# Later block transposes of e, and x turned on VectorE: two changes to attention followed by an MLP mixer on one core

## The chip, the core and the metric

The kernel runs on one NeuronCore of a Trainium2 chip. Five engines work side by side, each through its own instructions in order: TensorE (PE: matrix products, and transposes against an identity), VectorE (DVE), ScalarE (ACT), GpSimd (POOL) and SyncE (SP), which here only issues DMAs. Semaphores order them. SBUF is the working memory of 128 partitions, PSUM holds the results of PE. The metric is the time of one execution on the device, in microseconds. Before the change its median over eight runs is 1392.33 us (1391.53 to 1393.89).

## The reference

Threshold attention over 8 batch rows, 8 heads, 576 tokens and 64 columns a head; then the heads are laid side by side to 512 columns, and an MLP mixer follows, first over tokens and then over channels.

```python
def _attn_ref(q, k, v, tau):
    scale = 1.0 / np.sqrt(q.shape[-1])
    scores = scale * np.matmul(q, k.transpose(0, 1, 3, 2))
    thresh = np.max(scores, axis=-1, keepdims=True) - tau
    scores = np.where(scores >= thresh, scores, -1000000000.0)
    scores = scores - np.max(scores, axis=-1, keepdims=True)
    attn = np.exp(scores)
    attn = attn / (np.sum(attn, axis=-1, keepdims=True) + 1e-09)
    return np.matmul(attn, v)

def _moe_ref(x, w_tok1, w_tok2, w_ch1, w_ch2):
    xt = x.transpose(0, 2, 1)                      # x: (8, 576, 512)
    h = np.maximum(xt @ w_tok1, 0.0) @ w_tok2      # 576 -> 256 -> 576
    u = x + h.transpose(0, 2, 1)
    h2 = np.maximum(u @ w_ch1, 0.0) @ w_ch2        # 512 -> 1536 -> 512
    return u + h2
```

## The kernel before

**Units.** Attention is cut into 144 units: a batch row b has two halves w of two head pairs, and a half has nine units t. Eight units take 128 queries of one head pair (two heads); unit t = 4 takes the last 64 queries of both pairs of the half. A loop (L534) runs over the units and some rounds more, and its source order is the order in which each engine gets its instructions (`manual_schedule`, L81). Round u does, in this order:

- `scores(u)` (L287): 8 or 16 products into two PSUM tiles sc, the maxima mx on DVE (L306), a bias on POOL.
- `norm(u-1)` (L327): reciprocals rr on DVE, e scaled by rr on POOL.
- for unit w = u-2 the turn of e. In batch row 0, `turn` (L345): PE transposes with copies by DVE or ACT. From batch row 1 on, `turn_blocks` (L361): one DVE transpose in 32x32 blocks of 128x1152 into T (L368), and after the second unit of a group (a group is two units, or the unit t = 4 alone) 16 DMAs on SP (L378), which move the blocks across partitions into eT. The product with v follows two rounds later.
- `fill(0.4)` (L566): MLP steps, see below.
- `weigh(u)` (L310): threshold by a Prelu and exponential on ACT, with three times `fill(0.2)` between.
- issues of q and k loads for a pair two ahead (L576), two DMAs in each of the first eight units of a half, on SP in batch row 0 and on ACT later; lq and lk have two buffers (L70). `prep` at t = 2 and t = 7 turns a loaded pair on DVE into qT and kT (L283).
- `values` (L390), for what is due: products with v into pv (L408, L413), copied by ACT into xT (L418), which holds x with columns on partitions, two batch rows in one tile.

Between these stand calls of `weight(n)` (L223). It loads a weight piece in 64-bit form on SP (L176) into one of four raw buffers and decodes it on ACT, DVE and POOL; L191, L193, L201, L205, L209 and L215 are that decoding. It ends near 190 us.

**MLP steps.** When the last product of a batch row is emitted, `push(b)` (L515) queues its MLP as a list of steps with costs in us, mixed with what is left of the list before; `fill(share)` emits steps worth that share of a quota per round. The quota spreads the list over UB - 1 = 17 rounds and keeps 45 us for the time after the next push. The steps are: five `turn_x(t)` (four PE transposes of xT into PSUM, L430, and an ACT copy into x_sb, L431, which has tokens on partitions and one buffer); two `tok1(m)` (five products of w1 and x_sb, L439, Relu into a on ACT, L440); eight `tok2(c, f)` (two products, L446, and an add into xT on DVE, L450); then for groups of 256 tokens twelve `ch1` (L468, Relu into g on ACT, L469) and eight `ch2` (transposes of u, L480, products, L484; the last one of four copies to o on DVE, L489, and stores on SP, L490). The products of the MLP share two PSUM buffers, ps_mm; pv, x and the transposes share two, ps_tr.

```python
        for i, step in enumerate(steps):
            n = 2 if i in (NT, NT + NTK) else 1
            todo.extend(old[:n] + [step])
            del old[:n]
        todo.extend(old)
```

Of the kernel before, what the change touches and what calls it, by code (L numbers as in the profile page):

```python
# [9 lines left out]
F32 = mybir.dt.float32  # L10
# [11 lines left out]
def kernel(  # L22
# [71 lines left out]
    VL = 4  # L94
    vlast = [const.tile([P, P], F32, name=f"vl{i}") for i in range(VL)]

    def load_qk(n, eng, part=None):


        b, p = pairs[n]  # L100
        if n not in loaded:
            loaded[n] = [ld.tile([P, S // 32, 32], F32, tag=tag, name=f"{tag}_{n}") for tag in ("lq", "lk")]
        for i in range(4) if part is None else (part,):
            h, c = divmod(i, 2)
            for src, t, on in zip((q, k), loaded[n], eng):
                on.dma_start(
                    out=t[32 * i : 32 * i + 32], in_=src[b, 2 * p + h, :, 32 * c : 32 * c + 32].rearrange("(n t) d -> t n d", t=32)
                )

    def load_v(n):  # L110

# [127 lines left out]
        weight(3 * i + 4 - steps_done)  # L239

    load_piece(0)
    load_qk(1, (nc.sync, nc.sync))
    load_v(0)
    for i in range(1, NRAW):
        load_piece(i)
# [29 lines left out]
    def in_blocks(b):  # L275
        return b > 0
# [84 lines left out]
    def turn_blocks(u):  # L361

        key, place, n = group_of(u)
        e = st.pop(u)
        if place == 0:
            Ts[key] = work.tile([P, NK * 2 * P], F32, tag="T", name=f"T_{u}")
        T = Ts[key][:, 0 : NK * n * P]
        nc.vector.transpose(  # L368
            out=T.rearrange("p (a c n x) -> p c a n x", a=4, c=NK, n=n)[:, :, :, place, :],
            in_=e.rearrange("p (c a x) -> p c a x", c=NK, a=4),  # L370
        )
        if place == n - 1:
            del Ts[key]
            eTs[key] = work.tile([P, NK * 2 * P], F32, tag="eT", name=f"eT_{u}")
            w = NK * n * 32
            for a in range(4):
                for i in range(4):
                    nc.sync.dma_start(  # L378
                        out=eTs[key][32 * a : 32 * a + 32, w * i : w * i + w], in_=T[32 * i : 32 * i + 32, w * a : w * a + w]
                    )  # L380
# [37 lines left out]
        nc.scalar.copy(out=x, in_=ps)  # L418


    def token_mlp(b):
        xT = xTs.pop(b)
        o = S * (b % 2)
        s = {}

        def turn_x(t):
            M = MT[t]
            ps = ps_tr.tile([P, MAIN], F32, tag="tr", name=f"tx_{b}_{t}").rearrange("p (c x) -> p c x", c=NP)
            for p in range(NP):
                nc.tensor.transpose(out=ps[0:M, p, :], in_=xT[:, p, o + t * P : o + t * P + M], identity=ident)  # L430
            nc.scalar.copy(out=x_sb[0:M, t, :], in_=ps[0:M].rearrange("q p d -> q (p d)"))  # L431

        def tok1(m):
            need(2)
            if m == 0:
                s["a"] = work.tile([P, NTK, DM], F32, tag="a", bufs=1, name=f"a_{b}")
            ps = ps_mm.tile([P, DM], F32, tag="mm", name=f"t1_{b}_{m}")
            for t in range(NT):
                nc.tensor.matmul(ps, lhsT=w1[:, t, P * m : P * m + P], rhs=x_sb[:, t, :], start=(t == 0), stop=(t == NT - 1))  # L439
            nc.scalar.activation(out=s["a"][:, m, :], in_=ps, func=AF.Relu)  # L440

        def tok2(c, f):
            need(6)
            ps = ps_mm.tile([P, HS], F32, tag="mm", name=f"t2_{b}_{c}_{f}")
            for m in range(NTK):
                nc.tensor.matmul(  # L446
                    ps, lhsT=s["a"][:, m, P * c : P * c + P], rhs=w2[:, m, HS * f : HS * f + HS], start=(m == 0), stop=(m == NTK - 1)
                )
            u = xT[:, c, o + HS * f : o + HS * f + HS]
            nc.vector.tensor_add(out=u, in0=u, in1=ps)  # L450

        steps = [(0.44, lambda t=t: turn_x(t)) for t in range(NT)]
        steps += [(4.3, lambda m=m: tok1(m)) for m in range(NTK)]
        steps += [(0.97, lambda c=c, f=f: tok2(c, f)) for c in range(NCC) for f in range(2)]
        return steps
# [59 lines left out]
    def push(b):  # L515
        nonlocal quota
        uT = xTs[b]
        steps, old = token_mlp(b), list(todo)
        todo.clear()

        for i, step in enumerate(steps):
            n = 2 if i in (NT, NT + NTK) else 1
            todo.extend(old[:n] + [step])
            del old[:n]
        todo.extend(old)
        for i in range(2) if b % 2 == 0 else range(2, (2 * S + GR - 1) // GR):
            todo.extend(channel_mlp(b - b % 2, uT, i))
        quota = (sum(c for c, _ in todo) - (KEEP if b else KEEP_FIRST)) / (UB - 1)

    prep(0)  # L530
    due = deque()
    b_now = 0
# [86 lines left out]
```

## Time and profile before

| what | us |
|---|---|
| median of eight runs | 1392.33 |
| the profiled execution | 1391.53 |
| its span in the trace | 1389.70 |
| rounds without MLP (batch row 0): first matmul at | 8.89 |
| last product of scores at | 1185.4 |
| last matmul ends near | 1385.9 |

The span is that of the instructions in the trace; 1.8 us of the execution lie around it. Groups of instructions that matter here, as busy us and mean ns of one:

```profile
L368 DVE STREAM_TRANSPOSE T<-e 128x1152 f32<-128x1152 f32 x126 | 172.5, 1369 | 16.4 <-DMA eT<-T 9.7
L418 ACT COPY xT<-pv 128x256 f32<-128x256 f32 x64 | 23.8, 372 | 161.9 <-PE pv L413 155.9
...
L446 PE MATMUL t<-w,a 128*128 128x288 f32 x256 | 76.4, 426 | 14.9 <-DVE xT L450 11.7
L439 PE MATMUL t<-x_sb,w 128*128 128x512 f32 x160 | 72.9, 602 | 0.7 <-ACT g L469 0.7
```

A line gives the source line, the engine, the operation, its output and input tiles with shapes and the count; then the busy time in us and the mean of one in ns; then how long the engine had idled before these instructions in total, and who ended most of that. Two further groups, from the list of all groups: the x transposes (L430) are 160 with 26.5 us busy, and the x_sb copies (L431) are 40 with 23.1 us. An engine that idles costs time only if it is the one that the others wait for, so the stretches have to be told apart before these figures mean anything.

### The profile page before, as it was taken

To read this page: it belongs to the slowest core of one execution; us is meant where nothing else is said; L and a number is where in the kernel's file an instruction comes from. 1 tells how busy PE (TensorE), PEld (TensorE's weight loads), DVE (VectorE), ACT (ScalarE), POOL (GpSimd) and SP (SyncE) were. 2 spreads that over 40 slices of the span, in tenths; PEclk is the share of its full clock that TensorE was granted. 3 is DMA by queue.
4 is the path that set the end of the run, shared out by engine and by line. 5 is a ranking of instruction groups with operands and counts; after the bars stand their busy time and mean duration, and the time that the engine had idled before them with its cause. 6 is when DMAs were issued, how large, how long until landed. Compare 5 with 4: busy or idle time off the path is not lost.

```text
span 1389.7 us, 19515 instructions
## 1 busy us (share of the span) xinstructions
PE 1324.9 (95%) x6866; PEld 831.3 (60%) x6866; DVE 586.4 (42%) x1009; ACT 590.5 (42%) x1328; POOL 359.3 (26%) x683
## 2 busy tenths in 40 slices
PE   6776799999999999999999999999999999999998
PEld 3444465646565666665766567565657566575675
DVE  5789874444444444434244444433343453101000
ACT  5776564444454344443444435353434444120110
POOL 4566553232222122212122222221221222000000
PEclk9997999999999999999999999999999999999999
DMA  6444754444444433433433444443433433300000
GB/s 134 99 111 124 189 142 120 107 121 94 106 117 108 106 87 96 109 86 77 111 85 91 105 96 102 99 105 78 100 92 89 103 74 86 84 8 16 8 8 23
DMA packets 257376, 128.34 MB, mean 92 GB/s; under 512 B 208064, under 2 KB 221376, under 8 KB 257280
## 3 DMA queue, kind: packets, MB, share of 16 engines
q1 hardware_dynamic: 131632, 111.46, 30.6%
q10 hardware_dynamic: 125648, 15.64, 7.1%
q8 instruction: 55, 0.90, 0.3%
q14 instruction: 41, 0.34, 0.1%
HBM read 43.25 MB, written 9.44 MB: 38 GB/s over the span
## 4 chain that ended last, share of the span: by engine, by line
PE 85%; DVE 6%; SPq 2%; DMA 2%; POOL 2%; ACT 1%; issue 1%; ACTq 0%; DVEq 0%; POOLq 0%
PE c L484 27%; PE c L468 25%; PE sc L301 11%; PE pv L413 7%; PE t L439 5%; PE t L446 3%; DVE mx L306 3%; PE pv L408 2%; SPq L378 2%; PE tx L430 1%; PE c L480 1%; PE pv_s L413 1%; DVE T L368 1%; DMA scratch<-in_moe_w_ch_dram 1%; ACT e L316 1%
## 5 line engine op out<-in xcount | busy, mean ns | idle before, releaser
L306 DVE TENSOR_REDUCE mx<-sc 128x1 f32<-128x576 f32 x288 | 204.7, 751 | 522.5 <-PE sc L301 520.5
L468 PE MATMUL c<-xT,wc 128*128 128x256 f32 (+1 forms) x1920 | 399.0, 361 | 1.1 <-ACT g L469 0.9
L484 PE MATMUL c<-wc,g 128*128 128x512 f32 x864 | 389.1, 596 | 0.0
L468 PEld LDWEIGHTS c<-xT,wc 128*128 128x128 f32 x1920 | 334.2, 190 | 70.9 <-issue 28.4
L307 POOL TENSOR_SCALAR bias<-mx,toff 128x1 f32<-128x1 f32 x288 | 80.1, 278 | 812.4 <-DVE mx L306 757.9
L316 ACT ACTIVATE e<-sc,bias 128x576 f32<-128x576 f32 x288 | 199.3, 740 | 157.6 <-POOL bias L307 157.2
L484 PEld LDWEIGHTS c<-wc,g 128*128 128x128 f32 x864 | 157.9, 190 | 175.3 <-issue 173.2
L469 ACT ACTIVATE g<-c 128x256 f32<-128x256 f32 (+1 forms) x240 | 86.8, 362 | 334.3 <-PE c L468 329.6
L334 POOL TENSOR_SCALAR e<-e,rr 128x576 f32<-128x576 f32 x288 | 219.3, 774 | 15.8 <-DVE rr L331 3.8
L323 ACT ACTIVATE e<-e,ntau 128x576 f32<-128x576 f32 x288 | 220.6, 771 | 0.0
L301 PE MATMUL sc<-kT,qT 64*128 64x288 f32 (+1 forms) x1280 | 190.4, 436 | 15.5 <-DVE kT L283 8.9
L368 DVE STREAM_TRANSPOSE T<-e 128x1152 f32<-128x1152 f32 x126 | 172.5, 1369 | 16.4 <-DMA eT<-T 9.7
L301 PEld LDWEIGHTS sc<-kT,qT 64*128 64x128 f32 (+1 forms) x1280 | 104.3, 180 | 91.1 <-issue 47.7
L413 PE MATMUL pv<-eT,lv 128*64 128x256 f32 x1024 | 124.5, 386 | 0.0
L413 PEld LDWEIGHTS pv<-eT,lv 128*64 128x64 f32 x1024 | 75.5, 139 | 37.8 <-issue 1.1
L418 ACT COPY xT<-pv 128x256 f32<-128x256 f32 x64 | 23.8, 372 | 161.9 <-PE pv L413 155.9
L489 DVE COPY o<-c 128x512 f32<-128x512 f32 x36 | 24.5, 680 | 160.8 <-PE c L484 160.8
L446 PE MATMUL t<-w,a 128*128 128x288 f32 x256 | 76.4, 426 | 14.9 <-DVE xT L450 11.7
L439 PE MATMUL t<-x_sb,w 128*128 128x512 f32 x160 | 72.9, 602 | 0.7 <-ACT g L469 0.7
L446 PEld LDWEIGHTS t<-w,a 128*128 128x128 f32 x256 | 45.3, 191 | 41.7 <-DVE xT L450 19.5
L450 DVE TENSOR_TENSOR xT<-xT,t 128x288 f32<-128x288 f32 x64 | 28.0, 440 | 80.4 <-PE t L446 80.2
L323 ACT ACTIVATION_READ_ACCUMULATOR e<-e,ntau 128x1 f32 x288 | 56.4, 196 | 0.0
(48 smaller groups left out, 604.3 us busy)
## 6 DMA issues: line engine op xcount, KB each, us to landing
eT<-T SPq DMA_DIRECT2D x896, 72.0 KB, 2.0
scratch<-in_moe_w_ch_dram SPq DMA_DIRECT2D x24, 512.0 KB, 4.1
lv<-in_v_dram SPq DMA_DIRECT2D x32, 288.0 KB, 3.4
out_dram<-o SPq DMA_DIRECT2D x36, 256.0 KB, 2.2
eT<-T SPq DMA_DIRECT2D x224, 36.0 KB, 1.9
lk<-in_k_dram ACTq DMA_DIRECT2D x108, 72.0 KB, 2.7
lq<-in_q_dram ACTq DMA_DIRECT2D x104, 72.0 KB, 2.1
lq<-in_q_dram SPq DMA_DIRECT2D x24, 72.0 KB, 3.4
```

Source lines behind the costliest of these rows:

```text
L301: nc.tensor.matmul(sc[h][rows, f, 0:HS], lhsT=qT[r, cols], rhs=kT[r, HS * f : HS * f + HS], start=True, stop=True)
L306: nc.vector.tensor_reduce(out=mx[:, c], in_=sc[h][:, :, 0:HS], axis=AX.XY, op=ALU.max)
L316: nc.scalar.activation(out=eh, in_=sc[h][:, :, 0:HS], func=AF.Prelu, bias=bias[:, h : h + 1], scale=SCALE, alpha=STEEP)
L323: nc.scalar.activation(out=eh, in_=eh, func=AF.Exp, bias=ntau, accum_out=rs[:, h : h + 1])
L334: nc.gpsimd.tensor_scalar(out=eh, in0=eh, scalar1=rr[:, h : h + 1], scalar2=1.0, op0=ALU.mult, op1=ALU.mult)
L368: nc.vector.transpose(out=T.rearrange("p (a c n x) -> p c a n x", a=4, c=NK, n=n)[:, :, :, place, :], in_=e.rearrange("p (c a x) -> p c a ...
L413: nc.tensor.matmul(to[r], lhsT=lv[:, j, :], rhs=eT[:, j], start=False, stop=(c == NI - 1), skip_group_check=True)
L439: nc.tensor.matmul(ps, lhsT=w1[:, t, P * m : P * m + P], rhs=x_sb[:, t, :], start=(t == 0), stop=(t == NT - 1))
L446: nc.tensor.matmul(ps, lhsT=s["a"][:, m, P * c : P * c + P], rhs=w2[:, m, HS * f : HS * f + HS], start=(m == 0), stop=(m == NTK - 1))
L468: nc.tensor.matmul(ps, lhsT=wc1[:, j, c, :], rhs=uT[:, c, GR * i : GR * i + n], start=(c == 0), stop=(c == NCC - 1))
L469: nc.scalar.activation(out=s["g"][:, j, 0:n], in_=ps, func=AF.Relu)
L484: nc.tensor.matmul(flat, lhsT=s["g"][:, j, P * t : P * t + P], rhs=wc2[:, j, :], start=False, stop=(j == NJ - 1), skip_group_check=True)
```

## The change

It has two named parts and three that come with them.

1. `turn_blocks(w)` is called after `fill(0.4)` instead of ahead of it (batch row 0 keeps its `turn` where it was).
2. For b > 1, x is no longer turned by `turn_x`. After the last product of each half of a batch row (p odd, c = 1), an entry goes to `moves`. One round later `turn_x_blocks` turns the half's two pairs of xT in 32x32 blocks by one DVE instruction of 128x1152 into xt (one buffer). In each of the four rounds after it `move_x` issues four DMAs, two on SP and two on ACT, that put the blocks into x_sb. One round later still, after the second half, `push(b)` queues the MLP, now without `turn_x` steps. The columns of x_sb stand in another order, so the copies of batch rows 0 and 1 and the Relu of `tok1` permute them.
3. lq and lk have one buffer. The q and k loads are issued in other rounds: what a pair needs in the rounds between two `prep` calls. Pair 1 is loaded in rounds 0 and 1 rather than ahead of the loop.
4. The quota after `push(1)` spreads its list over UB + 4 = 22 rounds, since the next push comes later.
5. The loop has six rounds more at its end.

```diff
-            loaded[n] = [ld.tile([P, S // 32, 32], F32, tag=tag, name=f"{tag}_{n}") for tag in ("lq", "lk")]
+            loaded[n] = [ld.tile([P, S // 32, 32], F32, tag=tag, bufs=1, name=f"{tag}_{n}") for tag in ("lq", "lk")]
...
     load_piece(0)
-    load_qk(1, (nc.sync, nc.sync))
     load_v(0)
...
+    x_read = {}
+
+    def x_in_blocks(b):
+        return b > 1
+
+    def x_columns(t, M):
+        return x_sb[0:M, t, :].rearrange("q (i p d) -> q p i d", i=4, p=NP)
+
+    def turn_x_blocks(b, w):
+        xt = work.tile([P, S // 32 * 64], F32, tag="xt", bufs=1, name=f"xt_{b}_{w}")
+        o = S * (b % 2)
+        nc.vector.transpose(
+            out=xt.rearrange("q (c p d) -> q p c d", c=S // 32, p=2),
+            in_=xTs[b][:, 2 * w : 2 * w + 2, o : o + S].rearrange("q p (c r) -> q p c r", r=32),
+        )
+        return xt.rearrange("q (c x) -> q c x", x=64)
+
+    def move_x(b, w, xt, i):
+        if w == 0 and i == 0:
+            assert b < 1 or x_read[b - 1]
+        for a in range(4):
+            n = len(range(a, S // 32, 4))
+            eng = nc.scalar if a % 2 else nc.sync
+            eng.dma_start(
+                out=x_sb[32 * a : 32 * a + 32, 0:n, P * i + 64 * w : P * i + 64 * w + 64], in_=xt[32 * i : 32 * i + 32, a::4, :]
+            )
...
-            nc.scalar.copy(out=x_sb[0:M, t, :], in_=ps[0:M].rearrange("q p d -> q (p d)"))
+            nc.scalar.copy(out=x_columns(t, M), in_=ps[0:M].rearrange("q p (i d) -> q p i d", i=4))
...
-        steps = [(0.44, lambda t=t: turn_x(t)) for t in range(NT)]
+        steps = [] if x_in_blocks(b) else [(0.44, lambda t=t: turn_x(t)) for t in range(NT)]
...
-            n = 2 if i in (NT, NT + NTK) else 1
+            n = 2 if len(steps) - i in (8, 10) else 1
...
-        quota = (sum(c for c, _ in todo) - (KEEP if b else KEEP_FIRST)) / (UB - 1)
+        quota = (sum(c for c, _ in todo) - (KEEP if b else KEEP_FIRST)) / (UB + 4 if b == 1 else UB - 1)
...
-    for u in range(len(units) + LAG + 4):
+    for u in range(len(units) + LAG + 10):
...
-            if in_blocks(key[0]):
-                turn_blocks(w)
-            else:
+            if not in_blocks(key[0]):
                 for i in range(3):
                     turn(w, i)
...
         if b_now:
             fill(0.4)
+        if back and in_blocks(key[0]):
+            turn_blocks(w)
...
-            m = n + 2 + t // 4
-            if t < 8 and m < len(pairs):
-                load_qk(m, (nc.scalar if b_now else nc.sync,) * 2, t % 4)
-                if t % 4 == 3:
-                    load_v(m)
+            when = {3: (2, 0, 2), 4: (2, 2, 4), 5: (2, 4, 6), 6: (2, 6, 8), 8: (3, 0, 3), 0: (1, 3, 6), 1: (1, 6, 8)}
+            if u == 0:
+                load_qk(1, (nc.sync, nc.sync), range(0, 3))
+            if t in when:
+                m, lo, hi = when[t]
+                if n + m < len(pairs):
+                    load_qk(n + m, (nc.scalar if b_now else nc.sync,) * 2, range(lo, hi))
+            if t in (3, 7) and n + 2 + t // 4 < len(pairs):
+                load_v(n + 2 + t // 4)
...
+        for m in list(moves):
+            at, b, qd = m
+            if u == at:
+                xts = turn_x_blocks(b, qd)
+            elif u < at + 5:
+                move_x(b, qd, xts, u - at - 1)
+            else:
+                moves.remove(m)
+                if qd == 1:
+                    push(b)
         while due and due[0][0] <= u:
             _, b, p, c = due.popleft()
             values(b, p, c)
-            if p == NP - 1 and c == 1:
-                push(b)
+            if c == 1 and p % 2:
+                if x_in_blocks(b):
+                    moves.append((u + 1, b, p // 2))
+                elif p == NP - 1:
+                    push(b)
```

More of the change, by code (lines that the diff above doesn't have):

```diff
@@ L95, with load_qk @@
     vlast = [const.tile([P, P], F32, name=f"vl{i}") for i in range(VL)]
-    def load_qk(n, eng, part=None):
+    def load_qk(n, eng, parts=range(8)):
         b, p = pairs[n]
         if n not in loaded:
-            loaded[n] = [ld.tile([P, S // 32, 32], F32, tag=tag, name=f"{tag}_{n}") for tag in ("lq", "lk")]
-        for i in range(4) if part is None else (part,):
+            loaded[n] = [ld.tile([P, S // 32, 32], F32, tag=tag, bufs=1, name=f"{tag}_{n}") for tag in ("lq", "lk")]
+        for part in parts:
+            i, which = divmod(part, 2)
             h, c = divmod(i, 2)
[L105 to L108, printed above, removed]
+            eng[which].dma_start(
+                out=loaded[n][which][32 * i : 32 * i + 32],
+                in_=(q, k)[which][b, 2 * p + h, :, 32 * c : 32 * c + 32].rearrange("(n t) d -> t n d", t=32),
+            )
     def load_v(n):
@@ L418, in values @@
         nc.scalar.copy(out=x, in_=ps)
+    x_read = {}
[19 more added lines that the diff above has]
+                out=x_sb[32 * a : 32 * a + 32, 0:n, P * i + 64 * w : P * i + 64 * w + 64], in_=xt[32 * i : 32 * i + 32, a::4, :]
+            )
     def token_mlp(b):
@@ L439, in tok1 @@
                 nc.tensor.matmul(ps, lhsT=w1[:, t, P * m : P * m + P], rhs=x_sb[:, t, :], start=(t == 0), stop=(t == NT - 1))
-            nc.scalar.activation(out=s["a"][:, m, :], in_=ps, func=AF.Relu)
+            nc.scalar.activation(
+                out=s["a"][:, m, :].rearrange("q (c i d) -> q i c d", i=4, c=NCC),
+                in_=ps.rearrange("q (i c d) -> q i c d", i=4, c=NCC),
+                func=AF.Relu,
+            )
+            x_read[b] = m == NTK - 1
         def tok2(c, f):
@@ L527, in push @@
             todo.extend(channel_mlp(b - b % 2, uT, i))
-        quota = (sum(c for c, _ in todo) - (KEEP if b else KEEP_FIRST)) / (UB - 1)
+        quota = (sum(c for c, _ in todo) - (KEEP if b else KEEP_FIRST)) / (UB + 4 if b == 1 else UB - 1)
     prep(0)
     due = deque()
+    moves = []
     b_now = 0
     LAG = 2
-    for u in range(len(units) + LAG + 4):
+    for u in range(len(units) + LAG + 10):
         on = u < len(units)
```

## The prediction

> **What bounds the kernel now.** I read the busy table and the slices first, then the stage table of busy time, then TensorE's (PE's) own timeline for its gaps, and last the queues. The first three lines below are from the page; the rest is the stage table, whose columns are stretch, length and busy time (count) of PE, weight loads, VectorE (DVE), ScalarE (ACT) and GpSimd (POOL).
>
> ```profile
> PE 1324.9 (95%) x6866; PEld 831.3 (60%) x6866; DVE 586.4 (42%) x1009; ACT 590.5 (42%) x1328; POOL 359.3 (26%) x683
> ...
> PE   6776799999999999999999999999999999999998
> ...
> DVE  5789874444444444434244444433343453101000
> ...
> 140.00:184.00 44.00, 35.67 (x162) 22.55 (x160) 37.62 (x61) 25.64 (x53) 25.08 (x29) 0.96 0.68 190
> 184.00:280.00 96.00, 95.67 (x524) 59.64 (x525) 51.26 (x82) 49.53 (x114) 34.62 (x62) 1.00 0.47 113
> 280.00:1200.00 920.00, 909.12 (x4815) 567.05 (x4814) 379.12 (x641) 397.85 (x909) 220.20 (x467) 1.00 0.40 97
> 1200.00:1385.90 185.90, 185.90 (x728) 120.56 (x727) 9.17 (x16) 22.03 (x57) 0.00 (x0) 1.00 0.06 19
> ```
>
> Two regimes. Up to 184 us PE has holes and DVE is at seven to nine tenths: attention of batch row 0, then the weights' decoding. From 184 us to the end PE is in work for all but 11.2 us (0.33 + 10.88 + 0), and nothing else is near full. There an instruction taken off PE is worth its spacing on PE, and one added to another engine costs nothing until PE waits for it. Before 184 us the opposite holds.
>
> Now what the change removes from PE: a group of four x transposes, among matmuls.
>
> ```profile
> 1220.62 1.99 PE L468 MATMUL c<-xT,wc 128*128 128x256 f32 x8
> 1222.45 0.60 PE L430 MATMUL tx<-ident,xT 128*128 128x128 f32 x4
> 1222.89 1.89 PE L468 MATMUL c<-xT,wc 128*128 128x256 f32 x8
> ```
>
> The group shows 0.60 us, but the next matmul starts 0.44 us after it began: matmuls overlap, so 0.44 us is its price. Third, PE's largest gap in the regime that it bounds, with the DVE instructions around it (start, length, in brackets the idle time before it and its releaser):
>
> ```profile
> 315.08 2.21 PE L446 MATMUL t<-w,a 128*128 128x288 f32 x8
> 315.19 1.42 DVE L306 TENSOR_REDUCE mx<-sc 128x1 f32<-128x576 f32 x2 [3.34 <-PE sc L301]
> ...
> 316.80 1.36 DVE L368 STREAM_TRANSPOSE T<-e 128x1152 f32<-128x1152 f32 x1
> ...
> 318.08 0.78 DVE L450 TENSOR_TENSOR xT<-xT,t 128x288 f32<-128x288 f32 x2
> ...
> 318.55 3.18 PE L446 MATMUL t<-w,a 128*128 128x288 f32 x12 [1.26 <-DVE xT L450]
> ```
>
> Two token products have filled both ps_mm buffers; the third waits for the add of the first, and on DVE that add stands behind the maximum and a block transpose of e. Last, what the issuing queues pay (ns min/median/max of one issue):
>
> ```profile
> L378 SPq DMA_DIRECT2D eT<-T x1120: 507/589/2050, 136.2 to 1209.8; - x187
> ...
> L106 ACTq DMA_DIRECT2D lq<-in_q_dram x104: 317/318/367, 108.5 to 1108.1; - x104
> ...
> L106 ACTq DMA_DIRECT2D lk<-in_k_dram x108: 317/530/2078, 1.2 to 1108.5; - x108
> ```
>
> **What the Trainium skill says.** "Perfetto Trace Analysis", section "Identifying the Most-Contended Engine": matmul busy share overstates how full PE is, because its instructions are pipelined. This trace agrees: 160 x transposes average 296 ns, yet four of them take 0.44 us. "VectorE: DVE Perf Modes", section "The three transpose paths": DVE turns only 32x32 blocks, TensorE a whole 128x128 to PSUM, so a DVE path must move blocks between partitions by another means; here that means is the L378 transfers, and L368 turns 128x1152 in 1.37 us. "DMA: Bandwidth & Descriptors", section "Issuing engines are not separate DMA queues": issuing from several engines saves only their time to issue. This trace agrees that issue is what is scarce: SyncE (SP) needs 10.01 us for 16 issues, at a DMA share of 0.40 in the main stretch. "Advanced Engine Details and Errata", section "Sequencer Loop": instructions may be queued while a control instruction runs. At 585.58 us an ACT issue of 0.32 us begins beside an activation at 585.61 us, so issue time and activation time overlap here.
>
> **The change part by part.**
>
> *x transposes.* Batch rows 2 to 7 lose 5 groups of 4 each: 30 x 0.44 = 13.2 us of PE. The other bound is the merged busy time, 26.5 x 120/160 = 19.9 us; I take 13.2, since spacing is what followers feel. Batch rows 0 and 1 keep theirs. With them go 30 ACT copies (L431, 582 ns): 17.5 us on an engine that isn't the bound, worth 0.
>
> *Turning x on DVE.* 12 instructions of 128x1152, nearest row L368: 12 x 1.37 = 16.4 us. Each stands at the end of a unit, ahead of the next maximum, where DVE idles 520.5/126 = 4.1 us on average, waiting for scores. Taken as 0; with the cover gone it costs up to 16.4.
>
> *Moving x.* 192 issues, half on SP, half on ACT, four in each of 4 units per half row (48 units). On ACT two issues take 2 x 0.53 = 1.06 us per unit, 51 us in all. They stand behind the unit's exponentials and loads and ahead of the pv copy, before which ACT idles 155.9/54 = 2.9 us. Behind a late issue wait that copy and then the g activations, for which PE waits once two PSUM buffers are full. In the built program an ACT issue may also wait for an earlier DMA of SP's, as loads already do (copies of xT waited 5.7 us in total, three times). On SP, nine units carry 80 eT issues x 0.589 = 47 us; 8 moves add 4.7. A unit lasts about 8.0 to 9.5 us, so 72 us at least: SP fits. An eT batch has nearly three units from its transpose to its product, some 24 us, for 1.4 + 10 + 2 us plus a backlog of at most one batch. I take 1.0 us for ACT and 0.5 for SP; bounds 0 and 51.
>
> *T behind the first 0.4 of the MLP work.* PE's gaps on "DVE xT L450" after 280 us: 1.26 + 1.60 + 0.88 + 0.79 + 0.50 + 0.50 = 5.5 us, at most one T (1.37) of each recoverable: 5.3. The steps shift against the units, so a few new ones may arise: I take 4.5, bounds 0 and 5.3. Before 184 us there are two more, 3.85 and 2.33 us; there SP's chain of eT batches and weight loads (126 to 185 us without a pause) holds the next work back, so 0, at most 2 x 1.37 = 2.7. T itself leaves later only where an add or an o copy stands in that share; the order on DVE shows T mostly at the same place between the same neighbours. What is late next is eT, with the slack above.
>
> *q and k loads.* lq and lk lose a buffer, so parts of pair 1 move behind the first weight pieces and each load ends nearer to its turn. For batch row 0, putting the last parts behind the same pieces: pair 1 issued at 21.0, turned at 24.5; pair 2 at 47.0 and 51.1; pair 3 at 67.8 and 71.1; pair 4 at 94.0 and 97.6. With 2.2 to 3.4 us to land, pairs 3 and 4 are the tight ones: 0.5 us, bounds 0 and 3. From batch row 1 on a unit and more lies between.
>
> *Pace and end.* The later push moves MLP work some six units later, and row 1's is spread over 22 units instead of 17. PE's load per unit falls to some 8 us there (my estimate: 2.7 attention, 5.3 MLP), still above ACT's and SP's. The six added rounds at the end issue only work that is due anyway: 0.
>
> Sum: -13.2 - 4.5 + 1.5 + 0.5 = -15.7 us. From the profiled run's own 1391.53 us (span 1389.7 plus 1.8 around it) that gives 1375.8; the median of the eight runs is 0.8 higher, so the forecast is **1376.6 us**.
>
> **The rivals.**
>
> *Only the transposes pay.* The token waits come back elsewhere (T now stands ahead of the adds of the later shares) and pacing or eT takes some more: 1392.3 - 13.2 = 1379.1, up to 1386 with 7 us of new PE gaps. For it: the gaps are short and depend on alignment. Against: T follows directly behind the maximum now, 3.2 us in a row, and the split breaks that row.
>
> *The start gains too.* The two waits of 3.85 and 2.33 us go and weight pieces 1 to 3, issued some 4 us earlier, pull the decoding forward: 6 us more, 1370. Against: SP without a pause in that stretch.
>
> *Slower: the moves on ACT reach PE.* In the 48 units ACT stands 1.06 us for two issues, and longer when the DMA before isn't home; PE's PSUM buffers fill. It decides from (13.2 + 4.5 - 0.5)/48 = 0.36 us of PE per unit; at half the issue time, 0.53, plus nothing else, 1375.1 + 25 = 1400 us. For it: lk issues of up to 2.08 us. Against: the idle 2.9 us and the overlap seen at 585 us.
>
> *No difference that shows.* Stalls of both kinds just eat the gain, 1389.5 to 1395 us (0.2%, 2.8 us either way, is about what a measurement can tell here). That the change doesn't do what it says is excluded: the built order has 10 groups of tx instead of 40.
>
> **How the numbers follow.** Forecast 0.60 (its own range 1371 to 1379), only the transposes 0.20, the start too 0.10, no difference 0.04, slower 0.06. Faster is 0.60 + 0.20 + 0.10 = 0.90. The range 1370 to 1386 holds the first three but for their edges and leaves out the last two.
>
> **What would show it.** tx matmuls 160 to 40, x_sb copies 40 to 10, 12 new DVE turns near 1.37 us, 96 new issues on each queue. PE busy down by 13 to 20 us; PE's idle between 280 and 1200 us down from 10.9 to some 7, with "PE t <- DVE xT" nearly gone from that stretch. PE continuously in work from about 184 us, give or take 2. Wrong, if PE waits for eT or x_sb by DMA by more than 2 us in total, if "ACT g" or "ACT xT <- DMA" grows by more than 5 us, or if the first 184 us shift by more than 3.

## The result and the profile after

The kernel after takes 1381.34 us (median of 11 runs, 1379.57 to 1386.8) against 1392.99 us of the kernel before on the same chip (31 runs, 1391.17 to 1395.41): a ratio of 0.9921, 95% interval 0.9912 to 0.993, or 11.0 us of 1393 us (9.8 to 12.3). The profiled execution was its longest, 1386.8 us with a span of 1385.0. Of a difference between two traces I therefore say, where it matters, whether the medians show it too. Every ratio below is to the kernel before on the same chip; a difference between the medians of two other kernels may carry up to 1.8 us of the chips, since the kernel before itself differs by that much between them (1392.99 to 1394.74).

The page's first lines:

```profile
PE 1318.2 (95%) x6746; PEld 826.0 (60%) x6746; DVE 600.9 (43%) x1021; ACT 572.9 (41%) x1298; POOL 358.1 (26%) x683
...
PE   6776799999989999999999999999999999999998
```

PE has its 120 matmuls fewer, and yet only 6.7 us less busy time; and its row of nines has an 8 where it had none: the twelfth of 40 slices, 381 to 415 us. The stage table says where (same columns as before: stretch, length, busy time and count by engine, then PE's granted clock, DMA share, GB/s):

```profile
184.00:280.00 96.00, 93.56 (x514) 59.54 (x514) 49.32 (x80) 49.30 (x113) 33.94 (x60) 0.98 0.51 124
280.00:420.00 140.00, 132.61 (x720) 78.18 (x719) 71.31 (x121) 66.67 (x149) 40.15 (x86) 0.99 0.49 120
420.00:560.00 140.00, 136.96 (x769) 87.07 (x767) 66.55 (x111) 64.36 (x151) 37.74 (x80) 0.99 0.49 118
560.00:1200.00 640.00, 638.52 (x3285) 400.07 (x3284) 260.59 (x431) 255.53 (x590) 144.00 (x304) 1.00 0.42 101
```

From 280 to 1200 us PE stood for 10.88 us before; now for 7.39 + 3.04 + 1.48 = 11.9 us. The waits that the change was to take away are gone, and others of the same size have come, in another place: 10.4 of the 11.9 us lie between 280 and 560 us. The table of PE's waits from 190 to 1200 us (line that waits, what it waits for, us in total, times, longest) names them:

```profile
PE pv L408 <- DMA x_sb<-xt: 4.5, 1, 4.5
PE pv_s L408 <- DMA eT<-T: 2.2, 2, 1.7
PE pv L408 <- DMA eT<-T: 1.9, 2, 1.6
PE c L503 <- DVE xT L485: 1.1, 2, 0.5
```

Before, "PE t <- DVE xT" led this table with 5.5 us. Now the products of attention (pv, pv_s) wait for transfers of eT; where the name is x_sb, which pv doesn't read, the move issued right behind eT's last block landed just as PE started. All of it happens between 290 and 455 us, while row 1's MLP work is being spread. SP's own timeline there (start, length, transfers in a row):

```profile
370.91 1.33 SPq L446 DMA_DIRECT2D x_sb<-xt  x2
372.35 10.76 SPq L378 DMA_DIRECT2D eT<-T  x16
383.43 1.45 SPq L446 DMA_DIRECT2D x_sb<-xt  x2
384.98 0.53 SPq L115 DMA_DIRECT2D lv<-in_v_dram  x1
385.56 1.34 SPq L446 DMA_DIRECT2D x_sb<-xt  x2
387.00 10.31 SPq L378 DMA_DIRECT2D eT<-T  x16
397.36 1.29 SPq L446 DMA_DIRECT2D x_sb<-xt  x2
```

Each starts within 0.4 us of the end of the last: in this stretch SP is never free. The last block transpose ahead of the second row of 16 is this one:

```profile
379.81 1.36 DVE L368 STREAM_TRANSPOSE T<-e 128x1152 f32<-128x1152 f32 x1
```

So T is ready at 381.17 us, and SP comes to it at 387.00, behind the first row, four moves and a v load. The row ends at 397.31 us; the last of its 16, begun at 396.73, takes 2.3 us to land, and eT is home at 399.0. PE had stood since 394.90 and takes up the product 0.4 us later:

```profile
392.16 2.74 PE L519 MATMUL c<-wc,g 128*128 128x512 f32 x6
399.39 0.65 PE L408 MATMUL pv<-eT,vl 128*64 128x256 f32 x4 [4.49 <-DMA x_sb<-xt]
```

The moves stand in this chain: the six ahead of the second row hold SP for 4.4 us (370.91 to 372.35, 383.43 to 384.98, 385.56 to 387.00), which is about PE's gap of 4.49 us.

ACT's timeline has the same event from the other side:

```profile
384.16 4.65 ACTq L446 DMA_DIRECT2D x_sb<-xt  x2
388.85 0.33 ACT L418 COPY xT<-pv_s 128x64 f32<-128x64 f32 x2 [6.58 <-DMA eT<-T]
```

Two issues that take 1.2 us elsewhere stretch over 4.65 us. The second of them starts at 388.22 us; in the trace it waits for a semaphore that SP's v load raises too, and that load, issued at 384.98 us, lands 3.2 us later, at 388.2. So an issue of ACT's can stand still for an earlier transfer of SP's, and ahead of the copy behind the two ACT's computing idled 6.58 us.

The gap costs more than itself. PE's clock in stretches of one us behind it:

```profile
400.00:401.00 1.00, 1.00 (x10) 0.74 (x7) 0.00 (x0) 0.00 (x0) 0.00 (x0) 0.65 0.85 270
401.00:402.00 1.00, 1.00 (x7) 0.66 (x5) 0.00 (x0) 0.00 (x0) 0.00 (x0) 0.50 0.30 72
402.00:403.00 1.00, 1.00 (x7) 0.24 (x3) 0.00 (x0) 0.00 (x0) 0.00 (x0) 0.50 0.04 7
403.00:404.00 1.00, 1.00 (x7) 0.81 (x8) 0.00 (x0) 0.37 (x1) 0.00 (x0) 0.64 0.58 143
```

PE counts as busy here, but at half clock: 0.35 + 0.50 + 0.50 + 0.36 = 1.7 us lost. The Trainium skill says as much in "TensorE: Matmul & The Clock Gate", section "HAM oscillation — how this bites in real kernels": idle gaps of PE above some 3.4 us throttle the clock. The trace agrees for the 4.49 us gap; but behind two gaps of 1.68 and 0.53 us at 450 us it shows half clock again, with 1.6 us lost, so shorter ones can do it.

**An account that keeps the terms apart.** In windows of 10 us I take PE's idle time (stretch less busy) and its clock loss (busy times one less PEclk). What is left of the span is PE's work at full clock. Below the first two rows stand the experiments that follow; all in us, from one profiled execution each.

| kernel | span | idle to 190 | clock loss to 190 | idle from 190 | clock loss from 190 | rest: PE's work |
|---|---|---|---|---|---|---|
| before | 1389.7 | 50.2 | 8.0 | 14.7 | 0.0 | 1316.8 |
| after | 1385.0 | 51.1 | 11.8 | 15.7 | 4.5 | 1301.9 |
| before_T_behind | 1381.5 | 50.4 | 8.6 | 6.7 | 0.0 | 1315.8 |
| before_loads | 1399.2 | 49.1 | 14.5 | 17.9 | 0.0 | 1317.7 |
| after_T_front | 1389.6 | 50.4 | 16.8 | 22.6 | 1.7 | 1298.1 |
| after_due3 | 1393.6 | 48.6 | 16.7 | 18.7 | 3.0 | 1306.5 |
| after_keep15 | 1378.7 | 48.5 | 10.0 | 13.4 | 0.0 | 1306.8 |
| after_moves_sp | 1403.4 | 47.5 | 16.8 | 29.4 | 8.9 | 1300.8 |
| after_moves_act | 1385.0 | 50.1 | 14.1 | 16.1 | 2.7 | 1302.0 |
| after_earlyloads | 1376.7 | 48.4 | 9.4 | 14.7 | 3.0 | 1301.2 |
| early_moves_pool | 1366.9 | 49.6 | 10.1 | 7.6 | 0.0 | 1299.6 |
| early_pace17 | 1401.1 | 48.4 | 9.9 | 30.3 | 7.5 | 1305.0 |
| keep15_early | 1379.6 | 51.4 | 8.4 | 15.0 | 0.0 | 1304.8 |
| pool_x_row1 | 1380.6 | 52.8 | 10.3 | 14.5 | 3.0 | 1300.0 |

So the transposes did leave PE: 1316.8 - 1301.9 = 14.9 us. The last column is 1315.8 to 1317.7 us in the three kernels with all x transposes on PE, but 1298.1 to 1306.8 in the others, so this 14.9 is good to some 5 us. And the kernel got back only 4.7 us of span in this run, because clock loss rose by 8.3 us and idle time, which part 1 should have cut, rose by 1.9.

### The profile page after: what moved, and what is told of

The parts are those of the page before. It is cut to its first block, busy times and chain, and to the rows that moved or that the text cites. A ratio compares the mean times of both kernels' runs of the same rounds, so it can differ in the third digit from the quotient of the medians.

```text
span 1385.0 us, 19527 instructions
## 1 busy us (share of the span) xinstructions
PE 1318.2 (95%) x6746; PEld 826.0 (60%) x6746; DVE 600.9 (43%) x1021; ACT 572.9 (41%) x1298; POOL 358.1 (26%) x683
## 4 chain that ended last, share of the span: by engine, by line
PE 84%; DVE 6%; SPq 4%; DMA 3%; issue 1%; POOL 1%; ACT 1%; DVEq 0%; ACTq 0%; POOLq 0%
PE c L519 26%; PE c L503 26%; PE sc L301 11%; PE pv L413 7%; PE t L469 4%; PE t L481 4%; SPq L378 4%; PE pv L408 3%; DVE mx L306 2%; PE c L515 1%; DMA eT<-T 1%; PE pv_s L413 1%; DMA scratch<-in_moe_w_ch_dram 1%; DVE wc L206 1%; DVE eT L359 1%
## 5 line engine op out<-in xcount | busy, mean ns | idle before, releaser
L368 DVE STREAM_TRANSPOSE T<-e 128x1152 f32<-128x1152 f32 x126 | 172.4, 1369 | 16.1 <-DMA eT<-T 9.5
```

What stands on the lines that cost most here:

```text
L368: nc.vector.transpose(out=T.rearrange("p (a c n x) -> p c a n x", a=4, c=NK, n=n)[:, :, :, place, :], in_=e.rearrange("p (c a x) -> p c a ...
```

## The experiments

### The parts one by one

**before_T_behind: the kernel before, with part 1 alone.**

```diff
-            if in_blocks(key[0]):
-                turn_blocks(w)
-            else:
+            if not in_blocks(key[0]):
                 for i in range(3):
                     turn(w, i)
...
         if b_now:
             fill(0.4)
+        if back and in_blocks(key[0]):
+            turn_blocks(w)
```

> The kernel before with the first part alone: the block transposes of e stand behind fill(0.4). Theory Q (the missing microseconds come from SP's queue: in the stage that row 1's slower pace sets, eT batches and x moves together arrive after PE wants them): most of the 5.5 us of PE waits on the add into xT goes, no new wait on eT over 1 us, time 3 to 5 us below before, about 1389. Rival T (the later transpose itself makes eT late): waits of PE on DMA eT of 3 us and more, time not below before.

1382.16 us (1379.94 to 1383.56, 5 runs), ratio 0.9921, interval 0.9908 to 0.9935. Part 1 alone gives as much as the whole change, and over twice the 3 to 5 us expected. PE's waits from 190 to 1200 us, but for one of 0.2:

```profile
PE t L446 <- ACT g L469: 1.7, 2, 0.8
PE c L468 <- DVE xT L450: 0.5, 1, 0.5
```

The kernel before had 10.6 us of such waits, of which I had counted the 5.5 us "t <- DVE xT". Gone are also most of the 4.9 us put down to "ACT g". Why these belonged to T is seen where token and channel steps alternate. The kernel before:

```profile
801.63 1.24 PE L446 MATMUL t<-w,a 128*128 128x288 f32 x4
...
802.70 1.05 PE L468 MATMUL c<-xT,wc 128*128 128x128 f32 x8
...
803.34 1.36 DVE L368 STREAM_TRANSPOSE T<-e 128x1152 f32<-128x1152 f32 x1
...
804.12 1.24 PE L446 MATMUL t<-w,a 128*128 128x288 f32 x4 [0.37 <-ACT g L469]
804.62 0.41 DVE L450 TENSOR_TENSOR xT<-xT,t 128x288 f32<-128x288 f32 x1
```

The same place with part 1:

```profile
797.60 1.24 PE L446 MATMUL t<-w,a 128*128 128x288 f32 x4
...
798.67 1.05 PE L468 MATMUL c<-xT,wc 128*128 128x128 f32 x8
...
799.31 0.43 DVE L450 TENSOR_TENSOR xT<-xT,t 128x288 f32<-128x288 f32 x1
...
799.66 1.37 DVE L368 STREAM_TRANSPOSE T<-e 128x1152 f32<-128x1152 f32 x1
...
799.80 1.24 PE L446 MATMUL t<-w,a 128*128 128x288 f32 x4
```

The two ps_mm buffers hold one t and one c. Before, the add that frees t's buffer stood behind T until 804.62; the next product took the buffer that the activation g freed before that, and so the 0.37 us was put down to ACT. With T behind it the add is done at 799.74 and PE goes on without a gap. A wait for a buffer that either of two engines could have freed is named after the one that did, not after the one that was late.

**after_T_front: the kernel after without part 1.** `turn_blocks(w)` goes back ahead of `fill(0.4)`.

> The changed kernel with the first part undone: transposes of e in front of the MLP steps again. Theory Q: PE's waits for eT and x_sb DMAs between 290 and 455 us stay at some 9 us (give or take 3), and waits on the add into xT return: about 1385. Rival T: waits on eT below 3 us, time 1376 to 1380.

1389.82 us (1389.13 to 1393.54, 9 runs), ratio 0.9979, interval 0.9967 to 0.9992. By the medians part 1 is worth 8.5 us here too; the 1385 us expected were too low. PE's waits put down to DVE's xT are 8.0 us, 1.1 in the kernel after. PE still waits for eT (pv 5.1 us, pv_s 2.9 us): these waits don't come from T being emitted later. That theory falls.

**before_loads: the kernel before with the loads' part alone** (one buffer, and the order of part 3).

```diff
-            loaded[n] = [ld.tile([P, S // 32, 32], F32, tag=tag, name=f"{tag}_{n}") for tag in ("lq", "lk")]
+            loaded[n] = [ld.tile([P, S // 32, 32], F32, tag=tag, bufs=1, name=f"{tag}_{n}") for tag in ("lq", "lk")]
...
+            when = {3: (2, 0, 2), 4: (2, 2, 4), 5: (2, 4, 6), 6: (2, 6, 8), 8: (3, 0, 3), 0: (1, 3, 6), 1: (1, 6, 8)}
```

> The kernel before with the third part alone: one buffer for lq and lk and the new rounds of the q and k loads. Theory Q: no difference, within 1.5 us of before. Rival L (the loads, each nearer to its turn, hold DVE and with it the start back): 3 to 5 us above before, with DVE waiting for lq or lk in the first 120 us.

1396.85 us (1393.11 to 1400.98, 14 runs), ratio 1.0025, interval 1.0015 to 1.0036: it costs 3.5 us (2.1 to 5.0). The scores of unit 27, counted from 0, begin at 193.4 us, not 187.6. One line each for the first 190 us, first the kernel before:

```profile
0.00:190.00 190.00, 139.82 (x864) 88.59 (x865) 152.05 (x276) 126.63 (x264) 108.81 (x159) 0.94 0.53 134
```

then before_loads:

```profile
0.00:190.00 190.00, 140.95 (x801) 86.86 (x802) 145.75 (x270) 121.31 (x252) 103.11 (x156) 0.90 0.51 128
```

PE is busy just as long and gets 63 matmuls less done, at a clock of 0.90 instead of 0.94. VectorE's named waits for lq and lk, 2.9 us before and 3.6 us here, don't show it; the account's clock loss does: 8.0 to 14.5 us. The profiled run was the longest of the 14, 4.1 us over their median, so these 6.5 us are more than a typical run loses.

**after_due3: the kernel after, with each product due three rounds after its last transpose instead of two.** For this the last-64-query groups get an eT buffer of their own, the pool `small` gives one of its six up, and the loop has a round more.

```diff
-                when = u + (2 if in_blocks(b) else 1)
+                when = u + (3 if in_blocks(b) else 1)
```

> The changed kernel with products with v due three rounds after their transposes instead of two from row 1 on (the last-64-query groups get a buffer of their own, the small pool has five buffers, one more round at the end). Theory Q: eT then has a round more, PE's waits for eT and x_sb between 290 and 455 us fall from 9.6 us to under 1, the granted clock there stays at 1.00, and the time is some 10 us below the changed kernel: about 1371. Rival A (the 96 issues on ACT, not eT, cost the time): waits of that kind shift to ACT's copies and g, time within 3 us of the changed kernel, 1378 to 1384.

1393.7 us (1388.19 to 1399.73, 14 runs), ratio 1.0005, interval 0.9992 to 1.0018. No wait on PE is put down to eT any more, yet the kernel is 12 us slower than the kernel after: PE now waits for ACT's exponentials (7.1 us from 190 us on) and for x_sb copies (2.7 us). ACT's timeline has a part of the reason:

```profile
452.29 4.08 ACTq L446 DMA_DIRECT2D x_sb<-xt  x2
456.41 0.37 ACT L418 COPY xT<-pv 128x256 f32<-128x256 f32 x1 [7.07 <-DMA x_sb<-xt]
```

More slack for eT takes the waits for it away, but the engine whose issues stand still makes new ones. Whether the smaller pool `small` has a part in them isn't known. The next runs go to the queues themselves.

### Which queue, and what pace

**after_moves_sp and after_moves_act: all sixteen moves of a half row on one queue.**

```diff
-            eng = nc.scalar if a % 2 else nc.sync
+            eng = nc.sync
```

> The kernel after with all 16 moves of a batch row's turned x issued by SP, none by ACT. If SP's queue is what is behind: eT and x_sb waits of PE grow from 9.6 us to 13 or more in 280 to 460 us and further ones appear behind it, time 1384 to 1390. If the coupling by ACT's issues (which stand still for SP's transfers while pv_s copies and exponentials queue behind them) is what costs: ACT's idle time put down to DMA x_sb and DMA eT falls from 38 us to under 15, PE's waits fall too, time 1375 to 1379.

1403.11 us (1399.53 to 1407.42, 6 runs), ratio 1.0068, interval 1.0049 to 1.0086: 22 us slower than the kernel after by the medians. PE's waits from 190 to 1200 us:

```profile
PE t L469 <- DMA x_sb<-xt: 9.6, 2, 5.0
PE pv L408 <- DMA eT<-T: 9.5, 3, 7.0
PE pv_s L408 <- DMA eT<-T: 5.1, 3, 3.1
```

ACT's waits for x_sb and most of those for eT are gone, as the second theory had it (18.8 us for lk take their place), but SP's shortage decides: 8 issues more per half row on SP (some 5 us in nine units) make these waits of PE's 24 us, from 8.6. With `eng = nc.scalar`:

> The kernel after with all 16 moves of a batch row's turned x issued by ACT, none by SP. If SP's own eight moves (0.6 us each, two a round) make eT late: the waits by DMA eT between 280 and 460 us fall from about 5 us to 2 or less, time 1376 to 1380 unless ACT pays. If ACT is the dearer place (its issues wait for SP's transfers, 4.65 us in one case, and e and g come late): PE's waits by ACT e and ACT g grow by 3 us or more, time 1383 to 1390. If both effects are small: 1380 to 1383.

1390.2 us (1386.83 to 1393.2, 9 runs), ratio 0.9978, interval 0.9969 to 0.9988: 9 us slower than the kernel after by the medians. (The profiled run is the fastest of the nine, that of the kernel after was its slowest, and both have a span of 1385.0 us, so the two traces don't show these 9 us.) PE's waits for eT fall to 0.4 us, so the moves on SP had been what made them. But ACT pays; its waits on transfers in the same stretch are led by

```profile
ACT xT L418 <- DMA x_sb<-xt: 96.9, 21, 6.9
ACT e L316 <- DMA x_sb<-xt: 21.5, 3, 8.4
```

and PE waits for ACT's g and e, 9.5 us together. The kernel after, with half on each, lies between the two shortages. Neither queue has room.

**after_keep15: less work held back, so longer units in row 1's stretch.**

```diff
-    KEEP = 45.0
+    KEEP = 15.0
```

> The kernel after with KEEP 15 in place of 45: of each row's MLP only 15 us are left over when the next row's is pushed, so row 1's 22 rounds get some 1.4 us more each, as do the first rounds of nothing else; the later rows' quota stays as it was (what comes in is what goes out). Theory P (the new waits for eT and x_sb come because row 1's work, spread over 22 rounds with 45 us held back, leaves its units shorter than SP's queue needs): PE's waits by DMA eT and DMA x_sb in 280 to 460 us fall from 9.6 us to under 4, the idle time of 280 to 560 from 10.4 to 5 or less, and with the dips of the clock behind the gaps the time falls by 6 to 10 us, to 1371 to 1376. Rival N (it is the number of issues on SP, 80 block moves and 8 x moves in nine units, whatever the units' length): the waits stay at 7 us or more and the time at 1379 to 1384. Rival K (the 45 us held back were what filled PE elsewhere): waits put down to ACT g and DVE xT behind 560 us grow by over 5 us, and the time is 1384 or more.

1381.24 us (1378.99 to 1381.96, 4 runs), ratio 0.9909, interval 0.9894 to 0.9923. What theory P says of the waits holds: the 20 units from unit 42 on take 163.1 us (300.4 to 463.5), not 141.6 (302.0 to 443.6), which is 8.2 us a unit instead of 7.1, and no wait of PE for eT or x_sb is left. The time it says doesn't: the median is the kernel after's. By the account the trace gives back 6.3 us of span: 2.3 us of idle time, 6.3 us of clock loss and 2.6 us of idle time ahead of 190 us, less 4.9 us that PE's work got longer. As the kernel after was profiled 5.5 us over its median, some of these 6.3 us are that run's own. Why the work got longer I haven't found; PE's idle time from 560 to 1200 us is also 3.1 us longer. So longer units take the waits away, and are no cure.

**after_earlyloads: batch row 0's q and k loads end one unit sooner.**

```diff
+            if not b_now:
+                when = {3: (2, 0, 3), 4: (2, 3, 6), 5: (2, 6, 8), 8: (3, 0, 4), 0: (1, 4, 8)}
```

> The kernel after with the q and k loads of batch row 0 ended one unit sooner each: pair n + 2 in units 3 to 5 by 3, 3 and 2 (before: 3 to 6 by 2), pair n + 3 in units 8 and 0 by 4 (before: 8, 0 and 1). Theory L (row 0's preps wait for loads that end one or two units later than in the kernel before, and this is the 3.5 us that the loads alone cost): VectorE's waits for lq and lk before 190 us fall from 3.6 to 2 us or less, the unit that started at 193.7 us starts at 188 to 190, time 1377 to 1379. Rival B (it is the single buffer of lq and lk, whose next load can't start before the last prep has read it, and no order within a row mends it): the shift at 190 us stays 5 us or more, time 1380 to 1383.

1379.19 us (1377.84 to 1381.98, 4 runs), ratio 0.9899, interval 0.9884 to 0.9914. Unit 27 begins at 186.3 us (193.7 in the kernel after), and the first 190 us read

```profile
0.00:190.00 190.00, 141.62 (x870) 89.83 (x871) 152.81 (x281) 126.93 (x266) 109.92 (x162) 0.94 0.53 134
```

with the clock and the count of the kernel before. VectorE's waits for lq fall from 2.3 to 1.3 us, those for lk to none. Theory L holds in the trace. The gain by the medians, 2.2 us, is small enough for the two intervals to overlap; the clock loss to 190 us backs it: 8.0 and 8.6 us in the two kernels with the old loads, 10.0 to 16.8 in the seven traces with part 3, 8.4 to 10.3 in the five with part 3 and early loads.

### A third queue

**early_moves_pool: early loads, and the moves on GpSimd.** The Trainium skill, "Perfetto Trace Analysis", section "What "DMA-bound" means", counts an issuing engine whose sequencer track is solid with DMA slices as a bound of its own, and its section "DMA Optimizations" says that balancing over sync, scalar and GPSIMD may help then. SP's track above is solid; of the other two, ACT has just shown that it can't take them.

```diff
-            eng = nc.scalar if a % 2 else nc.sync
+            eng = nc.gpsimd
```

> The kernel with the early loads, and all 16 moves of a batch row's turned x issued by GpSimd, none by SP or ACT. Theory Q (there is no room left on SP's queue, and ACT's issues stand still behind SP's transfers): with the moves on a queue that issues nothing else, PE's waits by DMA eT and x_sb between 280 and 460 us fall from about 9 us to 2 or less, the idle time of 190 to 560 us from 9.8 to 4 or less, the dips of the clock there go too (2.8 us), and the time falls from 1379.2 to 1369 to 1373. Rival G (an issue on GpSimd is dearer than one on SP, no run so far shows its price, and 277 ns bias and 772 ns e of the softmax queue behind it): PE's waits by ACT e grow by 4 us or more and the time is 1379 to 1388.

1370.42 us (1368.7 to 1372.0, 4 runs), ratio 0.9828, interval 0.9816 to 0.9841. Theory Q's time comes true; PE's waits for eT are 2.3 us where it said 2 or less. An issue takes 0.57 us on GpSimd (median of 192), about what SP pays, and none of PE's waits from 190 us on is put down to GpSimd. PE from 190 us on:

```profile
190.00:560.00 370.00, 366.36 (x2018) 227.94 (x2017) 187.41 (x314) 181.31 (x416) 140.00 (x282) 1.00 0.50 122
560.00:1200.00 640.00, 639.75 (x3246) 397.06 (x3245) 253.90 (x419) 247.59 (x571) 217.70 (x435) 1.00 0.40 98
```

3.6 + 0.3 us of idle time are left, and the clock never drops. Against after_earlyloads, which differs from it in this one line, the account gives -7.1 us of idle time and -3.0 of clock from 190 us on, -1.6 of work and +1.9 before 190: -9.8 us of span, and -8.8 us between the medians. About so much the moves had cost on SP and ACT. It isn't that the transfers of eT got quicker: from 280 to 460 us they land 2.1 us after their issue in both kernels (1.9 for the groups of 64 queries). The moves also leave by another DMA queue there (q0 in its page), and no run parts the issuing engine from that queue. By the medians the kernel is 11 us faster than the kernel after.

**early_pace17: early loads, row 1's work over 17 rounds again.**

```diff
-        quota = (sum(c for c, _ in todo) - (KEEP if b else KEEP_FIRST)) / (UB + 4 if b == 1 else UB - 1)
+        quota = (sum(c for c, _ in todo) - (KEEP if b else KEEP_FIRST)) / (UB - 1)
```

> The kernel with the early loads, and row 1's MLP spread over 17 rounds as before, not over 22. Theory P (22 rounds make row 1's units shorter than SP's queue needs): row 1's units get some 29 percent longer, the eT and x_sb waits between 290 and 455 us fall from about 9 us to 3 or less; row 2 begins with less left over and gets some 1.7 us less a round, so a part of the waits may come back there, 3 us or less. Time 1373 to 1377. Rival N (the number of issues decides): the idle time of 190 to 560 us stays at 8 us or more, time 1378 to 1382. Rival E (the work runs out before the x of row 2 is there, as one expects of the reason for 22): PE stands without MLP work for some rounds, waits by ACT e of 5 us or more around 440 to 470 us, time above 1382.

1401.28 us (1398.55 to 1402.87, 6 runs), ratio 1.0044, interval 1.0031 to 1.0057: 22 us slower than after_earlyloads by the medians, 20 by the ratios. P and N miss; E has the direction, but its reason only in small part, since PE's waits for e are 4.6 us in all and lie elsewhere too. Row 1's stretch is better at first (from 280 to 420 us PE stands for 1.2 us). The trouble comes one row later:

```profile
460.00:500.00 40.00, 35.08 (x212) 21.97 (x213) 13.16 (x22) 16.65 (x43) 8.39 (x18) 0.96 0.49 112
500.00:540.00 40.00, 36.17 (x222) 23.19 (x219) 23.66 (x42) 17.59 (x40) 11.86 (x26) 1.00 0.51 121
540.00:580.00 40.00, 35.64 (x184) 22.84 (x184) 17.84 (x29) 19.77 (x46) 10.89 (x23) 0.96 0.51 121
580.00:620.00 40.00, 33.27 (x171) 18.71 (x168) 17.51 (x29) 15.20 (x33) 10.37 (x22) 0.94 0.50 121
```

19.8 us of idle time in 160 us, and the same waits return: eT 6.3 us, x_sb 3.5 and one of 4.4 on a transfer named lk. I had put 3 us on that. My reading, which no run tests, is that row 1 used up work that would have been left for row 2's list, so that the quota spreads that list thinner. Part 4 of the change, which I had priced at 0, holds off some 20 us once the push comes later.

**keep15_early: both of the above cures, without GpSimd.**

> KEEP 15 and the early loads together. If the two gains add up (early loads 2 us by the medians; KEEP 15 nothing by the medians, 4.5 us of waits and 4 us of clock by the traces): 1375 to 1379, idle time of 190 to 560 us about 5 us. If KEEP 15 loses elsewhere what it gains in row 1: 1379 to 1381.

1380.7 us (1379.76 to 1382.34, 4 runs), ratio 0.9903, interval 0.9891 to 0.9916. The gains don't add up; what KEEP 15 loses elsewhere is the second case of the expectation.

**pool_x_row1: early_moves_pool carried one batch row on.**

```diff
-        return b > 1
+        return b > 0
...
-/ (UB + 4 if b == 1 else UB - 1)
+/ (UB + 4 if b == 0 else UB - 1)
```

> The kernel with early loads and the moves on GpSimd, carried one batch row on: row 1's x too is turned by VectorE and moved (5 more groups of transposes off PE, 16 more moves on GpSimd), and so it is row 0's MLP that is spread over 22 rounds and row 1's over 17. By the trace accounts 30 groups gave about 14 us of PE's work, so 5 give 2.3: with PE's idle time behind 190 us still under 6 us, 1367 to 1369. Rival: row 1's units of 190 to 300 us, now shorter by 5 rounds in 22, meet eT's transfers and the loads on ACT, as row 2's did in the kernel after: idle time of 190 to 420 us grows by 4 us or more, with dips of the clock, 1371 to 1378.

1381.87 us (1380.68 to 1383.41, 5 runs), ratio 0.9917, interval 0.9903 to 0.993: the rival has the direction, and the time is 4 us above its range. PE from 190 to 420 us:

```profile
190.00:420.00 230.00, 221.69 (x1173) 133.50 (x1172) 119.94 (x198) 110.71 (x248) 97.68 (x194) 0.99 0.51 125
```

8.3 us of idle time, 3.1 in early_moves_pool, on eT (4.7 us), e (1.5) and xT (2.1): the 15 units from unit 27 on take 6.7 us each (185.0 to 286.0 us), not 7.2. PE's work at full clock didn't fall: 1300.0 us after 1299.6. It looks as if a queue of their own for the moves isn't enough where units are as short as that; but the edit also moves the longer spread from row 1 to row 0, and no run parts the two.

## Why the prediction was right, and where it was not

The forecast of 1376.6 us lies 4.7 us under the median, and the sum of -15.7 us stands against -11.0. That it came so near is owed to errors of opposite sign. By its own steps:

- *x transposes, -13.2 us: right.* PE's work at full clock fell by 14.9 us between the two traces, by 10 to 19 in the others with x off PE; no run has this part alone.
- *T behind the MLP work, -4.5 us, bounds 0 and 5.3: mechanism right, size wrong.* It is -11 us alone by the ratio (-8.2 of span between the traces), -8.5 inside the kernel after. The term was summed over gaps named "DVE xT" only. Gaps named "ACT g" of the same step had the same cause, as the pair of timelines shows.
- *x turns on DVE, 0: right.* 12 of 1.35 us; PE's waits for xT are 1.1 us.
- *Moves, 1.0 us on ACT and 0.5 on SP: this step failed.* The sentence "SP fits" used a unit of 8.0 to 9.5 us. In row 1's stretch it was 7.1 us, nine of them 64 us, and SP needs 47 us for eT and 5 for moves only on average: 16 issues come in one piece of 10 us, and between two such pieces stood four moves and a v load. An average that fits doesn't say that the latest of them is in time. The slack of an eT batch, "some 24 us", failed with it: for the product at 399.39 us PE was free 15.1 us after the last transpose had begun (379.81 to 394.90), and eT landed after 19.2 us, 5.8 of which T lay waiting for SP. On ACT an issue took 0.60 us, not 0.53; there the coupling to SP's transfers was named, at 5.7 us of old waits, but not priced: ACT's copies of xT waited 49 us for transfers (23.6 for x_sb, 14.6 for eT, 7.0 for lq, 3.9 for lk). In place of 1.5 us it was about 9 by the medians (early_moves_pool against after_earlyloads), part of it lost clock, a term that the sum didn't have.
- *q and k loads, +0.5 us, bounds 0 and 3: too small.* 3.5 us alone (2.1 to 5.0). Pairs 3 and 4 were named as the tight ones, rightly; the price was that of the waits, and in the trace the larger part is PE's lost clock, 6.5 us more.
- *Pace and end, 0: not tested as a price.* No run has this part alone. Undoing it costs some 20 us, so the change needs it; and the estimated "some 8 us" of a unit, measured 7.1, fed the error of the moves' step.

The time falls into the rival "only the transposes pay" (1379.1 to 1386), yet its story is the wrong way round: T paid, and the transposes' gain was eaten. Of the warnings set down for "wrong" all three came: PE waited for eT and x_sb for 8.6 us, not under 2; "ACT xT <- DMA" grew from 5.7 to 49 us; the first units shifted by 6 us. The slower rival, moves on ACT that reach PE, is what after_moves_act shows in part, at 9 us and not at 25.

What stays open: why PE's work is 4.9 us longer with KEEP 15, and how far the parts interact. By the medians T alone gives 11 and the loads take 3.5, which leaves 3.5 us for x and the pace together; without T they and the loads gain 2.9. Why the kernel after's runs differ by 7 us isn't known either. Their mean granted clocks differ with them: 0.983 to 0.985 in its runs above 1384 us, the profiled one among them, and 0.986 to 0.989 in those below 1383; by my estimate from these figures that is some 4 us of a run of 1385. after_earlyloads, profiled within 1 us of its median, shows the same waits.

## What to carry to other kernels

Price a queue by its longest row of issues against the shortest unit of the stage, not by sums over the whole kernel: a few moves of 0.6 us each were dear where 16 issues in a row already took more than a unit's time, and nearly free on an engine with an empty queue. When either of two engines could have freed a buffer, look at which one was late, since the name in the table is only that of the one which came first. And when a change makes units shorter, price the gaps together with the clock that PE loses behind them.

## What the runs showed of the hardware

- A PE gap can cost 1.7 us more than its length: half clock for some 3.4 us. It was seen behind a gap of 4.49 us, and behind 1.68 and 0.53 us shortly after each other; single gaps of 1.26 and 1.60 us in the kernel before left no dip. The length of the gap alone doesn't decide: in after_moves_act the clock dipped behind a gap of 2.71 us at 1066 us and not behind one of 2.68 us at 747 us, and in pool_x_row1 it dipped behind one of 1.32 us at 620 us.
- A transfer of 32 partitions issued on GpSimd took 0.57 us of the engine (0.55 to 0.79), about SP's 0.59 to 0.62, and landed 2.1 us later, as those of SP do after 2.0 to 2.1.
- Issues on ACT and SP were not independent in this program: two issues of ACT's, 0.6 us each, stretched over 4.65 us, the second starting as a v load of SP's landed (388.2 us), and the engine's computing stood behind them.
